# Loading the first batch uncast on another queue, with zero-tile matmuls in its gaps and a new instruction order

## The chip, the cores and the metric

The kernel runs on one core of one Trainium2 chip. The metric is device time in microseconds (us); a kernel's time is the median of its runs. Before the change that is 284.3 us (three runs: 283.76, 284.3 and 285.63).

The core's engines are named as in the profile: PE (TensorE, matrix products; PEld is its loading of weights), DVE (VectorE), ACT (ScalarE), POOL (GpSimd) and SP (SyncE, which here only issues transfers). Sixteen DMA engines move data between the chip's memory (HBM) and the core's SBUF. A transfer that is issued by SP goes into a hardware queue (q1 in the profile), one issued by POOL into a software queue (q0). In this kernel only POOL's transfers change the type on the way.

## The reference

Linear attention with cosine weights over 8 batches of 8 heads, 576 positions and 64 features a head, followed by a two-layer network with a squared ReLU on the 4608 resulting rows of 512:

```python
def _attn_ref(q, k, v):                      # each (8, 8, 576, 64) float32
    theta = np.pi / 2.0 * pos / S
    phi = lambda x: concat([max(x, 0) * cos(theta), max(x, 0) * sin(theta)], -1)
    kv = einsum('bhsf,bhsd->bhfd', phi(k), v)
    z = sum(phi(k), axis=2)
    num = einsum('bhsf,bhfd->bhsd', phi(q), kv)
    den = einsum('bhsf,bhf->bhs', phi(q), z)[..., None] + 1e-06
    return num / den
def _moe_ref(x, w_in, w_out):                # w_in (512, 2048), w_out (2048, 512)
    r = max(x @ w_in, 0.0)
    return (r * r) @ w_out
```

Inputs and output are float32; the kernel computes products in bf16.

## The kernel before

**Tiles.** The 576 positions of a batch are 512 "main" ones (four j of 128 partitions) and a tail of 64; a partition holds positions 4p to 4p+3, so that one head's piece of a load is 1 KB of float32 in HBM. The matrices work on units u: units 0 to 7 are the main rows of one batch each, unit 8 the tails of all batches. The first matrix product (G, in the table of operations; `first_plain` for units 0 and 1, `first_seven` with seven products of halves after) writes banks X, Y and E; ReLU goes to `rt`, the square to `gT`, and the second product (`second_plain`, `second_seven`, `last_seven`) makes the output rows in `ysb`, which SP writes out.

**A batch's attention** goes through these steps: load k, q, v; features phi of k and q (`kqp`; two instructions for each j, cosine and sine, on DVE, line 398, or ACT, line 402); values copied beside a column of ones (`vx`); the products kv (line 490) and their copy `kvz`; q's features transposed (`qpT`), on PE with a copy in the first three batches, by a transposing DMA of SP after; numerators with the denominator beside them, `den`, its reciprocal, and the quotient `x`; `x` transposed to `xT`.

**Batch 0 is cut in two halves of four heads** (`load_half`, `features_half`, `values(0, half)`, `kv_half`, `q_transpose_half`, `numerators_half`, `x_transpose_half`), since nothing else can run yet. k's first half is loaded by SP in float32 into `ysb`, which no result needs yet. The other halves are cast to bf16 on the way into `kqin` and `vin`, by POOL: v, q, then k, v, q (in two quarters) of the second half. The small tails come between. Then POOL loads w_in in four parts of 1 MB of float32 (`load_w1`), batch 0's q tail and batch 1's q, k and v. A later batch's load into `kqin` has to wait until the features of the batch before have been read.

The first quarter of unit 0's G is cut by token block and by half of the contraction, so that its pieces can begin when the first heads are done (line 862 with 128 x 128 outputs); the other three quarters need all of batch 0's `xT`.

**Order.** Operations are collected in a list (`add`), each with the engines it may run on, what it reads and writes. `Plan.order` takes them in the order that `TABLE` spells out by hand: a number is the operation's place in the list, `+` selects its second engine, and `<n` gates a transfer until operation n has ended. The costs and due times given to `add` (`xfer`, `late`, `hold`, `at`) were used to make the table and do nothing when the kernel is built. Engines work in order, so the table's order on one engine decides who waits behind whom.

Before anything has landed, PE runs 17 matmuls of a zero tile (`warm`).

Of the kernel before, what the change touches and what calls it, by code (L numbers as in the profile page):

```python
# [11 lines left out]
F32 = mybir.dt.float32  # L12
# [66 lines left out]

BOTH = [3, 4, 5, 6, 7]  # L80
# [8 lines left out]
ORDER2 = 'kvq23'  # L89
TABLE = """  # L90
0 1 2 3 5 4 6 7 8 9 29+ 26+ 27+ 10 23+ 11 28+ 30 31 12 24 25 19+ 22 20 13 32 21 33 34 35 36 37
14 15 41 44+ 43 40 45+ 42 16 48 47 83+ 46 55 81 79+ 80 17 76 78+ 49 82+ 50 18 62 56+ 51 52 77+
38 57 84 63+ 53 85 39 58 86 54+ 87 59 88 89 90 64 91 60 69 65+ 70+ 66 93+ 61 71 92+ 67 72 73 100
68 101+ 95 148 94 158 98 97+ 99 102 107 96 103+ 114 137 108+ 104 153 154 115+ 121 149 109 74 110
75+ 111 122+ 105 116 106+ 117 123 159 118 112 150 113+ 155 124 125 119 151 120+ 152+ 126 156 127
163 157+ 164 165 166 160 167 161 169 162 410 170 129 128 130 138 171 131 139 132 140 172 175 133
134 211+ 141 173 209 210 176 214 142 215 135 213+ 219 216 143 168 182 174 221+ 144 180 212 220+
177 145 222 181 146 178 183 223 147 224 187 218 179 199 225 197 188 198 184 202 226+ 203 217
227+ 200 189 411 185 196+ 228 413 193 201+ 229 230 231 239 205 204 191 206 232+ 207 186+ 240 208
233 234 241 235 236 237 242 238+ 136+ 286 192 243 194 244 250 190 280 251 245 252 195+ 275 246  # L100
255 281 256 257 253 254+ 260 258 261 287 262 259+ 247 340+ 248 418 265 337+ 263 266 299 249 267
336+ 276 264+ 338 341 300 339 268 334 270 343 269+ 306 344 342+ 271 272 301 307 419 273 333 312
274+ 302+ 335+ 415 297 376<302 349+ 313+ 308 350+ 298+ 377<313 352+ 319 346 378<298 348 347+ 345
354 303 351+ 356 353+ 420 282 357+ 379<356 422 355+ 288 304 380<422 358+ 277 381<288 421 382<288
359 310 423 360+ 383<421 361+ 305 289 311 362 320+ 384<305 278 363+ 290+ 364+ 283 279+ 309 412
365 314+ 317 366 367 368 315 369 284 318 370 285 316+ 371 372 373 531 535+ 374 321 532 534 375
324 541 536+ 538 385 537 291 539 322 533 292 323+ 386 553<386 387 293 425 414 390 325 326 544
391 392 330 327 395 294 396 397 328 295 331+ 400 329 388 545 429 389 332+ 430 401 402 431 432
416 405 393 433 540 398 426 296 554<540 399+ 434 394+ 435 555<540 406 436 407 556<406 403 428
439 408 557<439 440 409+ 441 542+ 558<440 404 442 469 471 467 559<469 444 468 472 445 470 547  # L110
443 548 476 446 477 543 417 473 560<543 474 427 561<417 478 475 447 479 549 550 448 551 480 486
552 424 481 483 482 562 484 449 487 450 563 485+ 564 491 437 492+ 489 565 689 493 490 566 567
451 494 488 438 686 496 568 495 569 497 501 570 498 571 502 546 452 499 506 504 507 500 503 505
572 508 453 573 516 574 509 455 688+ 456 685 575 510 511 457 687 512 513 691 698 517 576 454 583
577+ 695+ 514 521 519 515 522 461 462 693+ 523 578 520 518 690 524 579 701 692 463 697+ 696 694+
702 707<463 623 526 525 625 527 708<526 703 621 464 626 622 709<621 528 624 704 710<528 529 630
628 631 530 711<529 705 627 629 712<705 458 706 580 632 713<530 459 584 633 585 714<584 582 586
640 715<586 587 716 581 635 717+ 598 636 599 634 641 600 718 601 643 465 645 644 719 602+ 466
637 646 655 699 638 647 593 639 648 642 720+ 840+ 594 700 649 595 596 721 839+ 603 460 604 597
722 842+ 588 650 841 605 651 850 652 851 849 656 589 653 590 852 660 654 591 661 658 592 723 606  # L120
659 724 725 662 607 657 663 844 670 848+ 843 726 665 846 727 609 728 666 610 671 611 664 729 612
845+ 608 675 673 613 676+ 861<608 667 674 615 668 847+ 616 677 669 862<668 672 678 863<677 730
779 679 731+ 864<669 617 732 618 865<679 680 733 619 682 866<680 681 775 855 856 780 776 857 853
858 778 859 777 784 860 683 737 785 782 684 614 781 783 854 786 870 734 787 794 738 789 735 620
739 790 740 795 747 736 748 741 799 788 797 800 749 871 798 872 742 801 867<742 791 802+ 873
868<791 809 792 804 869<809 793 750 805 752 810 753 874 754 875 743 751 812 877 813 814 878 755
879 815 796 756 744 803 994+ 824 993 816 996 880 995+ 806 998 881 757 882 817 758 759 1000+ 807
883 760 819 808 761 745 820 884 876 811 825 885 886 763 997+ 764 818 887 827 762 829 828+ 821
830 1006 765 999 746 766 822 831 823 769 832 1007 770 1005+ 826 1003+ 771 833 772 1004+ 929 891
930 834 1002 836 1001 835 931 933 837 1009 934 1010 1011 838 1012 938 936 1015<938 939 773 935  # L130
937 892 932 1016<773 888 940 1017<932 1013 941 893 1018<1013 948 767 890 943 1014 894 1019<948
944 889 901 1020<890 949 902 1021<901 903 895 942 953 951 1022<953 954 904 952 1023<951 945 955
946 963 956 905 1024 896 947+ 906 1025 958 1026 950 907 959 957 908 964 1027 897 1028 1029 968
960 969 1148 966 1030 1151 909 967 961 1031 970 910 1032 1033 774 898 1158+ 899 1008 1157 965
962+ 1150 1034 971+ 978 911 972 912 913 900+ 914 1035 1036 973 915 975 974 1149 1045 1037 1152
917 979 916 918 976 983 981 984 977 923 982 1038 985 1155+ 1039 980 1040 986 919 924 987 988
1154 1087 1083 989 990 1084 1088 925 1147 926 1085 1160 991 1092 1090 1093 992 1163 1164 1165
1094 1153 920 1086 1095 1046 1159 927 921 1047 1091 1156 1048 922 1089 1161 1049 1166 1096 1097
1102 1042 1098 1050 928 1103 1051 1052 1044 1105 1107 1106 1043 1167 1099 1108 1055 1168 1100
1117 1109 1101 1169 1110 1060 1061 1170 1171 1112 1056 1113 1104 1118 1172 1111 1062 1173+ 1063  # L140
1174 1122 1064 1114 1123 1175 1057 1115 1176 1120 1177 1116+ 1178 1124 768 1119 1125+ 1065 1066
1126 1121 1127 1179 1128 1053 1180 1181 1132 1054 1058 1133+ 1067 1182 1068 1059 1137 1069 1135
1162 1138 1070 1129 1136 1071 1130 1139 1041 1077 1131 1140 1134 1232 1141 1072 1142 1144 1143
1078 1145 1233 1079 1228 1190 1146+ 1229 1080 1231 1234 1230 1235 1081 1237 1236 1187 1073 1082
1238 1074 1191 1075 1188 1192 1193 1239 1189 1194 1247 1240 1183 1200 1241 1242 1195 1243 1196
1248 1244 1205 1245 1252 1206 1246 1253 1207 1250 1254 1251 1201 1255 1208 1249 1209+ 1257 1256
1262 1258 1202 1263 1203 1197 1204 1198 1267 1199 1259 1184+ 1268 1210 1185 1211 1260 1186 1269
1265 1261 1270 1264 1266 1212 1271 1213 1272 1214 1277 1273 1215 1274 1216 1278 1275 1217 1282
1276 1279 1283 1280 1335 1284 1281 1333 1222 1334 1285 1223 1336 1337 1286 1287 1218 1288 1289
1338 1224 1290 1225 1342 1226 1219 1343 1291 1340 1220 1339 1341 1344 1221 1292 1295 1076 1345  # L150
1296 1227 1297 1293 1352 1347 1305 1346 1348 1306 1294 1353 1298 1349 1299 1355 1350 1357 1310
1351 1358 1311 1312 1356+ 1359 1307 1360 1354 1367 1361 1362 1313 1363 1364 1368+ 1308 1300
1314+ 1301 1365 1372 1315 1366 1373 1316 1317 1374 1309 1370 1375 1369 1371 1318 1376 1377 1319+
1382 1378 1379 1383 1302 1380 1303 1387 1381 1385 1388 1321 1386 1384 1304 1389 1322 1390 1323
1391 1324 1392 1320 1325 1394 1393 1401 1326 1395 1327 1328 1396 1329 1330 1402 1331 1430 1403
1397 1431 1332 1404 1432 1405 1398 1433 1406 1434 1408 1407 1438 1400 1435 1439 1437 1436 1409
1410 1399 1411 1412 1440 1413 1441 1414 1442 1415 1443 1416 1444 1417 1420 1445+ 1418 1419 1421
1446 1449 1447 1448 1425 1426 1422 1424 1450 1423 1427 1454 1451+ 1428 1429 1455 1453 1452 1456
1457 1458
"""  # L160
RATE0 = RATE = 0.37
LLATE = TLATE = HOLD = 0.0
DEN_ACT = (0.16, 0.27)
BASE1, BASE, SHIFT0, PERIOD, KZ0, KZ1, NUM0, NUM1 = (0.0,) * 8


@with_exitstack
def kernel(
# [202 lines left out]
    def load_w1(i):  # L371
# [3 lines left out]
            lambda eng: eng.dma_start(  # L375
                out=w1[:, :, f0:f1], in_=moe_w_in[:, f0:f1].rearrange("(kb p) f -> p kb f", p=P)
            ),
            [("w1", i)],
        )

    def load_w2(i):
# [979 lines left out]
```

## Time and profile before

| | us |
|---|---|
| median of three runs | 284.3 |
| the profiled execution | 286.11 |
| its span, first to last instruction | 284.3 (284.25) |
| PE busy | 268.3 (94%) |
| DVE busy | 225.8 (79%) |
| ACT busy | 183.5 (65%) |
| POOL busy | 60.3 (21%) |
| PE busy in the first 7.0 us, the next three stretches of 7.0 us | 5.32, 1.88, 4.89, 6.11 |

"Busy" is the time in which an engine had an instruction of the program at work; matmuls overlap in the pipeline, so PE can be busy all the time at either clock. The clock is the share of full speed that the throttle granted to PE: in this execution it is one half from 11.04 us to 24.7. A DMA share is the sum of the packets' own times over sixteen engines; it can be over one, since an engine has several packets under way. GB/s counts bytes as they are written, so a load that casts to bf16 reads twice as many.

Where the first transfers went in this execution (issue, and landing of the last byte as the instructions that wait see it):

```
k half 0      SP    0.74    4.65
v half 0      POOL  1.25    6.47
k, v tails    POOL  2.60 to 4.43    6.66 to 7.36
q half 0      POOL  5.03    9.66
k half 1      POOL  6.39   13.82
v half 1      POOL  7.15   15.13
q half 1      POOL  7.89, 8.62   15.86, 16.66
w_in          POOL  9.35 to 11.55   19.17, 21.69, 24.23, 26.82
batch 1's q   POOL 22.55   29.87
```

### The profile page before, as it was taken

What the parts mean: (1) busy time and instruction counts of PE and PEld (TensorE: products, weight loads), DVE (VectorE), ACT (ScalarE), POOL (GpSimd) and SP (SyncE); (2) the same over time, 40 slices, a digit from 0 to 9 for tenths busy, and PEclk for the clock granted to TensorE, in tenths of its full rate; (3) what the DMA queues carried; (4) which work ended last, traced back from release to release, by engine and by line L of the source; (5) the groups of instructions that cost most, each with busy time, mean ns of one, the idle gap of its engine ahead of it and who ended that gap; (6) DMA issues with size and microseconds to landing.
All of it is one profiled execution on the core that took longest, in us unless ns stands there. A gap on an engine that the chain in (4) does not pass through costs nothing.

```text
span 284.3 us, 6995 instructions
## 1 busy us (share of the span) xinstructions
PE 268.3 (94%) x2851; PEld 228.9 (81%) x2851; DVE 225.8 (79%) x443; ACT 183.5 (65%) x311; POOL 60.3 (21%) x92
## 2 busy tenths in 40 slices
PE   7278999999999999989999999999999999999994
PEld 2157886777789988968899888989898888888883
DVE  1465795977889899988999997998888768878662
ACT  5275779888866897677547878765576556544430
POOL 8711638262124006201420035000000000000000
PEclk9757999999999999999999999999999999999999
DMA  9999499999499856999999869928442100320134
GB/s 133 150 207 162 48 181 196 193 195 181 98 179 187 111 113 90 178 176 230 144 205 155 130 109 166 183 65 166 135 125 54 74 2 10 140 84 2 74 113 111
DMA packets 81951, 37.34 MB, mean 131 GB/s; under 512 B 50688, under 2 KB 79872, under 8 KB 81920
## 3 DMA queue, kind: packets, MB, share of 16 engines
q0 software_dynamic: 42288, 18.09, 52.4%
q1 hardware_dynamic: 38992, 18.29, 30.1%
q10 hardware_dynamic: 640, 0.52, 0.7%
q8 instruction: 22, 0.36, 0.5%
q14 instruction: 9, 0.07, 0.1%
HBM read 36.70 MB, written 9.44 MB: 162 GB/s over the span
## 4 chain that ended last, share of the span: by engine, by line
PE 87%; DMA 6%; POOL 2%; DVE 2%; ACT 1%; issue 1%; POOLq 0%
PE psY L915 13%; PE psY L1068 12%; PE psX L915 8%; PE psE L915 8%; PE psX L1068 8%; PE psE L1068 8%; PE psX L862 4%; DMA qpT<-kqp 3%; PE psA L490 3%; PE psA L671 3%; PE psY L862 3%; PE psE L862 3%; DMA kqin<-in_k_dram 3%; PE psX L1019 2%; PE psY L1142 2%; PE psA L566 2%
## 5 line engine op out<-in xcount | busy, mean ns | idle before, releaser
L1068 PEld LDWEIGHTS <-gT 128*128 128x128 bf16 x448 | 43.3, 98 | 5.2 <-issue 0.2
L915 PEld LDWEIGHTS <-w 128*128 128x128 bf16 x448 | 42.7, 98 | 4.9
L1068 PEld LDWEIGHTS <-gs 128*128 128x128 bf16 x336 | 32.4, 98 | 3.7
L915 PEld LDWEIGHTS <-w1s 128*128 128x128 bf16 x336 | 32.1, 98 | 3.8
L915 PE MATMUL psX<-xT,w 128*128 128x256 bf16 x224 | 33.6, 273 | 0.0
L915 PE MATMUL psY<-ts,w 128*128 128x256 bf16 x224 | 33.6, 273 | 0.0
L831 DVE TENSOR_TENSOR gT<-rt 128x2048 bf16<-128x2048 bf16 x26 | 31.8, 1223 | 1.9
L827 ACT ACTIVATE rt<-psY 128x512 bf16<-128x512 f32 x35 | 20.9, 598 | 18.9 <-PE psY L915 17.4
L1068 PE MATMUL psX<-w,gT 128*128 128x256 bf16 x224 | 30.0, 273 | 0.1
L862 PEld LDWEIGHTS <-w 128*128 128x128 bf16 x288 | 25.9, 101 | 2.8 <-issue 0.2
L827 ACT ACTIVATE rt<-psX 128x512 bf16<-128x512 f32 x35 | 21.0, 600 | 7.9 <-PE psX L915 5.4
L405 ACT COPY p1u<-psY 128x512 f32<-128x512 f32 x26 | 15.2, 586 | 16.8 <-PE psY L915 13.8
L957 DVE CUSTOM_DVE_ANT_0 rt<-psE,p1u 128x512 bf16<-128x512 f32 x28 | 19.2, 686 | 6.7 <-PE psE L915 6.6
L957 DVE CUSTOM_DVE_ANT_0 rt<-psE,p1v 128x512 bf16<-128x512 f32 x28 | 19.2, 686 | 6.1 <-PE psE L915 3.5
L405 ACT COPY psY<-psX 128x512 f32<-128x512 f32 (+1 forms) x35 | 19.4, 559 | 6.4 <-PE psX L1142 3.0
L337 POOL DMA_DIRECT2D kqin<-in_k_dram x7 | 6.5, 926 | 72.1 <-PE psX L915 18.5
L405 ACT COPY p1v<-psY 128x512 f32<-128x512 f32 x25 | 14.7, 586 | 9.6 <-PE psY L915 9.3
L699 DVE TENSOR_TENSOR x<-psA,rden 128x512 bf16<-128x512 f32 x28 | 19.4, 691 | 1.1
L833 ACT ACTIVATE gT<-rt 128x2048 bf16<-128x2048 bf16 x10 | 19.1, 1911 | 0.7 <-DVE rt L957 0.5
L915 PE MATMUL psE<-ts,w1s 128*128 128x256 bf16 x112 | 16.8, 273 | 0.0
L915 PE MATMUL psE<-xT,w1s 128*128 128x256 bf16 x112 | 16.8, 273 | 0.0
L915 PE MATMUL psY<-ts,w1s 128*128 128x256 bf16 x112 | 16.8, 273 | 0.0
(152 smaller groups left out, 549.1 us busy)
## 6 DMA issues: line engine op xcount, KB each, us to landing
out_dram<-ysb SPq DMA_DIRECT2D x16, 512.0 KB, 3.4
kqin<-in_q_dram POOLq DMA_DIRECT2D x7, 512.0 KB, 8.1
kqin<-in_k_dram POOLq DMA_DIRECT2D x7, 512.0 KB, 6.6
vin<-in_v_dram POOLq DMA_DIRECT2D x7, 512.0 KB, 8.6
w<-in_moe_w_in_dram POOLq DMA_DIRECT2D x4, 512.0 KB, 12.5
w<-in_moe_w_out_dram POOLq DMA_DIRECT2D x4, 512.0 KB, 9.3
ysb<-in_k_dram SPq DMA_DIRECT2D x1, 512.0 KB, 3.9
vin<-in_v_dram POOLq DMA_DIRECT2D x2, 256.0 KB, 6.6
```

What stands on the lines that cost most here:

```text
L337: return lambda eng: eng.dma_start(out=dst[:, :, js, :], in_=s[:, :, js, :])
L405: (nc.vector.tensor_copy if e == "DVE" else nc.scalar.copy)(out=dst, in_=src)
L490: nc.tensor.matmul(out=psA[:, half, hh * E1 : (hh + 1) * E1], lhsT=lhsT, rhs=rhs, start=(j == 0 and hh == 0), stop=(j == J and hh == HH - 1),)
L671: nc.tensor.matmul(out=dst, lhsT=lhsT, rhs=kz[:, half * HH + hh, :], start=True, stop=True)
L699: nc.vector.tensor_tensor(out=xv[:, i : i + m], in0=n4[:, :, :, 0:D].rearrange("p b (k l) d -> p b k l d", l=2), in1=rd_[:, i : i + m] .re ...
L827: nc.scalar.activation(out=dst, in_=src, func=ACTF.Relu)
L831: nc.vector.tensor_tensor(out=dst, in0=src, in1=src, op=ALU.mult)
L833: nc.scalar.activation(out=dst, in_=src, func=ACTF.Square)
L862: nc.tensor.matmul(out=bank[bk][:, hh * W + c0 : hh * W + c1], lhsT=w1[:, kb, (h0 + hh) * P : (h0 + hh + 1) * P], rhs=x_block(u, t, kb)[:, ...
L915: nc.tensor.matmul(out=acc[:, hh * W : (hh + 1) * W], lhsT=lhs[:, kk, c : c + P], rhs=rhs(kk), start=start and hh == 0 and kk == 0, stop=T ...
L957: nc.vector._custom_dve(dve_ops.TENSOR_ADD_SAT, out=dst, in0=wide(acc), in1=wide(part), s0=INF, s1=0.0)
L1068: nc.tensor.matmul(out=acc[:, pr * W : (pr + 1) * W], lhsT=lhs[:, hb, pr * P : (pr + 1) * P], rhs=rhs[:, hb, :], start=start and pr == 0 a ...
```

## The change

All of batch 0's main inputs are issued by SP, in float32, one after the other (k, v, q of the first half, k, v, q in two quarters of the second), and stay float32 in SBUF: the first half's in the three buffers of `ysb`, the second half's in the second buffer of `gT`. Features and value copies of batch 0 read them there. POOL issues the tails of k and v first, then makes the positions (`iota`) and the identity, and then loads w_in; the last of its four parts is gated by the end of the warm-up matmuls. `W1HOLD` marks w_in's loads with `hold`, which has no effect beyond the table. Batch 0's main inputs no longer use `kqin` and `vin`, so batch 1's q can be issued right behind.

Six operations of zero-tile matmuls into bank E (`fill`, 26 matmuls in all) are added at six places of PE's order: 12 after the warm-up, then 2, 5, 1, 5 and 1 between batch 0's steps.

The whole table is a new one, also for the later units. On batch 0 it shares features and copies out anew: the value copies of batch 0 are on ACT, and DVE begins with the tails' features. In the built program ACT's first second-half q features wait for the first quarter that SP loads last but one, and one of ACT's and one of DVE's wait for SP's last load; DVE's stands ahead of all numerators of the second half, and ACT's ahead of the copy of kvz's second half.

```diff
@@ -77,6 +77,7 @@
         return got
 
 
+W1HOLD = (0, 1, 2, 3)
 BOTH = [3, 4, 5, 6, 7]
 SECOND7 = 1
 FIRST7 = 2
@@ -87,76 +88,77 @@
 PEQ = (0, 1, 2)
 PEX = (0, 1, 2)
 ORDER2 = 'kvq23'
+FILL = (12, 2, 5, 1, 5, 1)
 TABLE = """
-0 1 2 3 5 4 6 7 8 9 29+ 26+ 27+ 10 23+ 11 28+ 30 31 12 24 25 19+ 22 20 13 32 21 33 34 35 36 37
-14 15 41 44+ 43 40 45+ 42 16 48 47 83+ 46 55 81 79+ 80 17 76 78+ 49 82+ 50 18 62 56+ 51 52 77+
...
+0 1 2 8 3 9 4 11 5 12 13 6 14 10 7 15 26+ 16 28+ 23+ 17 1459 25+ 20 19 18<0 24+ 27+ 38 22+ 31+
+39 30+ 21 29 32 42 45+ 33 34 43 35 40+ 36 41 55 37 47 48 46 44+ 1460 56 49+ 57 69 81+ 58 50 62
...
 """
 RATE0 = RATE = 0.37
 LLATE = TLATE = HOLD = 0.0
@@ -235,7 +237,17 @@
     kin, qin = kqin[:, 0], kqin[:, 1]
     kint, qint = kqint[:, 0], kqint[:, 1]
     vin, vint = sb("vin", [P, H, J, D]), sb("vint", [P, HH, D])
-    k0 = ysb[:, 0:2].rearrange("p a i c -> p (a i c)").rearrange("p (h j d) -> p h j d", h=H, j=J)
+
+    def uncast(nm, half):
+
+        n = "kvq".index(nm)
+        if half == 0:
+            flat, ks = ysb[:, n].rearrange("p i c -> p (i c)"), [("y", n, i) for i in range(2)]
+        else:
+            flat = gT[1][:, 4 * n : 4 * n + 4, :].rearrange("p b c -> p (b c)").bitcast(F32)
+            ks = [("g", 1, 2 * n + i) for i in range(2)]
+        return flat.rearrange("p (h j d) -> p h j d", h=HH, j=J), ks
+
     kqp, kqpt = sb("kqp", [P, 2, J, H, F]), sb("kqpt", [P, 2, HH, F])
     kp, kpt = kqp[:, 0], kqpt[:, 0]
     qp = [kqp[:, 1, 2 * i : 2 * i + 2] for i in range(2)]
@@ -350,14 +362,12 @@
     def load_half(nm, half, js=range(J)):
 
         hs, jj = slice(half * HH, (half + 1) * HH), slice(js[0], js[-1] + 1)
-        first = nm == "k" and half == 0
-        src, dst = {"k": (k, k0 if first else kin), "v": (v, vin), "q": (q, qin)}[nm]
+        src, (dst, _) = {"k": k, "v": v, "q": q}[nm], uncast(nm, half)
         s = src[0, hs, 0:MAIN, :].rearrange("h (p j) d -> p h j d", j=J)
-        wr = [("y", a, i) for a in range(2) for i in range(2)] if first else []
         load(
-            f"{nm}0", "SP" if first else "POOL", 0.5 if first else 0.9, 0.53 * len(js) / J,
-            lambda eng: eng.dma_start(out=dst[:, hs, jj, :], in_=s[:, :, jj, :]),
-            [(nm, j, "h", half) for j in js] + wr,
+            f"{nm}0", "SP", 0.5, 0.53 * len(js) / J,
+            lambda eng: eng.dma_start(out=dst[:, :, jj, :], in_=s[:, :, jj, :]),
+            [(nm, j, "h", half) for j in js],
         )
 
     def load_tail(nm, b, eng="POOL"):
@@ -375,7 +385,7 @@
             lambda eng: eng.dma_start(
                 out=w1[:, :, f0:f1], in_=moe_w_in[:, f0:f1].rearrange("(kb p) f -> p kb f", p=P)
             ),
-            [("w1", i)],
+            [("w1", i)], hold=HOLD if i in W1HOLD else None,
         )
 
     def load_w2(i):
@@ -425,18 +435,15 @@
 
     def features_half(nm, j, half):
         hs = slice(half * HH, (half + 1) * HH)
-        first = nm == "k" and half == 0
-        if nm == "k":
-            src, dst = (k0 if first else kin)[:, hs, j, :], kp[:, j, hs]
-        else:
-            src, dst = qin[:, hs, j, :], qp[j // 2][:, j % 2, hs]
+        src, ks = uncast(nm, half)
+        dst = kp[:, j, hs] if nm == "k" else qp[j // 2][:, j % 2, hs]
         for c, col in ((0, cos_col), (1, sin_col)):
             add(
-                f"{nm}f0.{j}", either((0.24, 0.33), FEATT[1]) if first else either(*FEATT),
+                f"{nm}f0.{j}", either((0.27, 0.355), FEATT[1]),
                 lambda e, c=c, col=col: feature(
-                    e, dst[:, :, c * D : (c + 1) * D], src, col[:, j : j + 1]
+                    e, dst[:, :, c * D : (c + 1) * D], src[:, :, j, :], col[:, j : j + 1]
                 ),
-                [(nm, j, "h", half), ("cs",)], [(nm + "p", j, c, "h", half)], bias=0.35,
+                [(nm, j, "h", half), ("cs",), *ks], [(nm + "p", j, c, "h", half)], bias=0.35,
             )
 
     def features_both(b, j):
@@ -458,16 +465,17 @@
             )
 
     def values(b, half=None):
-        hs, m = (slice(0, H), 1) if half is None else (slice(half * HH, (half + 1) * HH), 0.5)
-        rd = (lambda j: [("v", j)]) if half is None else (lambda j: [("v", j, "h", half)])
+        hs = slice(0, H) if half is None else slice(half * HH, (half + 1) * HH)
+        src, ks = (vin, []) if half is None else uncast("v", half)
+        rd = (lambda j: [("v", j), *ks]) if half is None else (lambda j: [("v", j, "h", half), *ks])
         wr = (lambda j: halves(b, ("vx", j))) if half is None else (lambda j: [("vx", j, "h", half)])
         for i in range(2):
             add(
-                f"vc{b}", either((0.33, 0.465), (0.935, 1.05)) if half is None else either((0.2, 0.33), (0.52, 0.63)),
+                f"vc{b}", either((0.33, 0.465), (0.935, 1.05)) if half is None else either((0.39, 0.475), (0.52, 0.62)),
                 lambda e, i=i: copy(
                     e,
                     vx[:, 2 * i : 2 * i + 2, hs, 0:D],
-                    vin[:, hs, 2 * i : 2 * i + 2, :].rearrange("p h j d -> p j h d"),
+                    src[:, :, 2 * i : 2 * i + 2, :].rearrange("p h j d -> p j h d"),
                 ),
                 rd(2 * i) + rd(2 * i + 1), wr(2 * i) + wr(2 * i + 1), bias=0.35,
             )
@@ -1225,13 +1233,19 @@
 
         return mm
 
+    def fill(n):
+        for _ in range(n):
+            nc.tensor.matmul(
+                out=bank["E"][:, :], lhsT=zeros[:, 0:P], rhs=zeros[:, :], start=True, stop=True
+            )
+
     add("warm", pe(0.31 * WARM), lambda e: warm(WARM, "warm")(), [], [("X",), ("E",)])
     load_half("k", 0)
-    load_half("v", 0)
+    load_tail("k", 0)
+    load_tail("v", 0)
     add("iota", [("POOL", 0.45, 0.5)], lambda e: const_pool(), [], [("sidx",), ("queue", "POOL")])
     add("cs", [("ACT", 0.4, 0.4)], const_act, [("sidx",)], [("cs",)])
-    load_tail("k", 0)
-    load_tail("v", 0)
+    load_half("v", 0)
     load_half("q", 0)
     add("ident", [("POOL", 0.4, 0.5)], lambda e: make_identity(nc, ident), [], [("ident",), ("queue", "POOL")])
     load_half("k", 1)
@@ -1319,6 +1333,10 @@
             weight_sums2()
         second(u)
 
+
+    for n in FILL:
+        add("fill", pe(0.22 * n), lambda e, n=n: fill(n))
+
     with tc.manual_schedule():
         for o in plan.order():
             o.fn(o.alts[o.eng][0])
```

## The prediction

> **What bounds the kernel now.** I read the page's forty slices first: where is PE, the engine with 94% of the span, not full, and what is full there?
>
> ```profile
> PE   7278999999999999989999999999999999999994
> PEclk9757999999999999999999999999999999999999
> DMA  9999499999499856999999869928442100320134
> ```
>
> A slice is 7.1 us. PE is short of nine tenths in the first three or four slices and in two more. In those first slices the clock is also down, and the DMA engines are full. Windows over the stages give the sizes (length, then busy time with instruction count of PE, weight loads, DVE, ACT and POOL, then clock, DMA share, GB/s):
>
> ```profile
> 7.00:14.00 7.00, 1.88 (x28) 1.29 (x28) 3.41 (x13) 1.89 (x5) 5.35 (x8) 0.79 1.28 147
> 14.00:21.00 7.00, 4.89 (x56) 3.81 (x57) 4.41 (x20) 5.10 (x13) 1.24 (x2) 0.50 1.26 205
> 21.00:28.00 7.00, 6.11 (x72) 5.60 (x71) 3.86 (x18) 4.11 (x10) 0.90 (x1) 0.74 1.26 171
> ...
> 118.00:128.80 10.80, 8.97 (x94) 7.85 (x91) 8.29 (x14) 7.27 (x12) 0.00 (x0) 1.00 1.33 195
> 128.80:280.00 151.20, 151.20 (x1565) 134.84 (x1564) 126.58 (x206) 90.58 (x152) 12.81 (x18) 1.00 0.60 111
> ```
>
> From 28.7 us to 280 PE has a single wait of its own, 1.83 us at 128.4 (on a transposing DMA). So the kernel is a start, batch 0's attention, whose length varies, and then 251 us of matmul work that the change does not lessen. The end follows the moment at which the dense stretch begins. I take for that moment the row in which PE begins the last piece of the first quarter of unit 0's first matrix (P0 below):
>
> ```profile
> 28.70 1.05 PE L862 MATMUL psX<-xT,w 128*128 128x128 bf16 x16
> ```
>
> What ends the waits before it? The chain of waits in order of time has one long piece there:
>
> ```profile
> 6.39 7.43 DMA kqin<-in_k_dram
> ```
>
> k's second half, issued by POOL at 6.39, lands at 13.82. Then v lands at 15.13, q's last quarter at 16.66 and w_in's four parts at 19.2, 21.7, 24.2 and 26.8. All of these are in POOL's single queue, so batch 0's inputs have the DMA engines before w_in does. From 16.66 to 28.7 batch 0 is bound by the engines' own chain.
>
> **The change, part by part.**
>
> *Issues.* POOL loses six issues of 0.75 to 0.89 us (4.7 us in sum). SP gains the six and issues seven in a row, each 0.47 as k's first half: 0.74 to about 4.0. SP's next work is at 69.9, so nothing stands behind them. POOL now issues k's and v's tails from 1.25 (0.62 each, to 3.75), sidx (0.43) to 4.2, ident (0.5) to 4.8 and w_in's four parts (0.73 each) to 7.7, where they had begun at 9.35. cos and sin move from 3.1 to about 4.65, hidden by k's landing at 4.65; without that cover 0 to 1.5 us of the first half, which is not on the path below. The gate of w_in's last part on the warm-up matmuls (over at 6.5) is passed when POOL reaches it at 7.0: 0. If it were late, batch 0's q tail and batch 1's q would queue behind it, needed only after 28 us.
>
> *Uncast data.* ACT's feature of 256 f32 elements takes 0.49 to 0.51, of bf16 the same: 0. DVE's takes 0.33 against 0.29: 13 of them, 0.5 us, in waits of DVE. Four copies of v's halves go from DVE (a pair 0.76) to ACT; no row has ACT reading 512 f32 from SBUF, the nearest are its 512 f32 from PSUM at 0.60 and DVE's pair, so 0.38 to 0.60 each; I take 0.55. They are hidden if the q behind them lands later, which it does below. The borrowed buffers cost nothing: the first result is written to ysb at 65.4, and gT's second buffer is filled later still.
>
> *Zero-tile matmuls.* 26 of them. Warm-up matmuls at full clock start 0.215 us apart: 5.6 us, at half clock 0.43: 11 us. PE is idle 9.8 us in the first 28. They cost nothing where PE waits for q, up to 5.6 if nothing is late.
>
> *The transfers.* Nothing is saved in bytes read from HBM; what changes is who shares the engines. Three rows price a packet: the f32 loads alone, w_in alone (read 2 KB, written 1 KB), and both queues at work (SP's 4 KB output rows beside POOL's loads).
>
> ```profile
> q1 hardware_dynamic: 335, 0.34, 101.0%
> ```
> ```profile
> q0 software_dynamic: 1028, 1.02, 122.8%
> ```
> ```profile
> q1 hardware_dynamic: 87, 0.36, 88.5%
> q0 software_dynamic: 98, 0.02, 22.6%
> ```
>
> The first is 1.0 us from 2.5: 16 x 1.01 us / 335 = 48 ns. The second is 5 us from 17: 96 ns. The third is 1.0 us from 71: 87 packets against 98, about one for one although SP's are 4 KB and POOL's 128 to 512 bytes; both shares together 1.11. POOL's loads were queued there (402 packets in the half microsecond from 85.5 show its pace when SP has little), so turns are taken by packets.
>
> Batch 0 has 5 x 512 packets of 1 KB and, in q's quarters, 1,024 of 512 bytes; w_in 2,048; the tails 1,024 of 128 bytes (31 ns). Up to 3.5 us SP's queue moves some 405 packets as now. Then tails one for one: 1,024 pairs x 79 ns / 16 / 1.11 = 4.6 us, to 8.1, when w_in has been issued for three microseconds. Left for SP's queue: 1,130 of 1 KB and 1,024 of 512 bytes, against 2,048 of w_in. They alternate to the end: (2,048 x 96 + 1,130 x 48 + 920 x 40 ns, the 40 between 31 and 48) / 16 / 1.11 = 16.2 us, to 24.3. So q's last quarter lands at about **24.6**, not 16.66; with the overlap that w_in alone shows (1.23) at 23. k's second half comes at 13.7 as now, v's at 17.9, q's first quarter at 21.6.
>
> *The new order behind it.* Two engines, each working in order, wait for that last quarter: DVE with the feature that stands ahead of all second-half numerators, ACT with another. Behind ACT's wait stand an xT copy, another feature and the copy of kvz's second half, without which no numerator starts. After 24.6: 0.43 + 0.37 + 0.5 + 0.38 = 26.3; eight numerators 0.6 (the clock is half, PE having waited); then PE's next in order, eight G0 matmuls (1.06) and four transposes (0.63), to 28.6; two qpT copies on ACT 1.14; numerators 0.5, to 30.2; and from the last numerator to P0 it was 26.34 to 28.70, 2.2 to 2.4. P0 at **32.4**, 7.8 after the landing. The nearest row for that distance is 6.7, from the last q feature's end (22.0) to P0; measured from ACT's last q feature (26.8) it gives 33.5.
>
> *The sum.* P0 moves from 28.7 to 32.4: +3.7. The later order was made anew; the trace says only that 1.8 us is to be had and nothing of what a new stall costs, so -1.8 to +1.8, taken as 0. The profiled execution took 286.11 (span 284.25, 1.86 around it), 1.8 above the median 284.3: 286.1 + 3.7 = 289.8 on its own terms, **288.0** on the median's.
>
> **Rivals.** All hang on one number, the landing L of q's last quarter: time = 284.3 + L + 7.8 - 28.7, as long as L is over about 15.7. No change is at L = 20.9.
>
> 1. *SP's queue is served first*, since its descriptors stand there before w_in's. Left at 8.1: 1,130 x 48 + 1,024 x 40 ns / 16 / 1.06 = 5.6 us, L = 14.1. Then ACT binds: to the end of batch 0 it has 22 features at 0.43, four value copies at 0.55, three qpT copies at 0.57, four xT copies at 0.37, two of kvz at 0.38 and one 0.27, 15.9 us from 4.7, plus 2.5 to 3 us of waits, P0 at 23.5: -5.2, **279.1**. It ends faster, from L under 18. For it: SP's seven issues come first, and POOL's load issued at 84.4, beside a put, had its first packet only at 87. Against: the 87 to 98 above, and the q transposes on SP's queue that took 9.8 us to land beside POOL's loads where the median is 5.3.
> 2. *Shared by bytes.* Half of 0.38 MB/us (that window's total) each: 1.64 MB / 0.19 = 8.6 from 8.1, with the landing L = 17.1, P0 at 24.9: -3.8, **280.5**. Against it the same rows, where SP had nine tenths of the bytes.
> 3. *POOL's packets get more turns.* From 141 to 143 us POOL moved 564 packets and SP's transposes 186. At two for one w_in is through at 21.9, and batch 0's q tails and batch 1's q, next in POOL's queue, go on taking two turns of three, 6 us more for q's quarters: L = 28, +7.1, **291.4**.
>
> The Trainium skill, DMA: Bandwidth & Descriptors, section Queues, rings and completion order, says that each engine goes round the queue rows packet by packet, with some 9 to 17 descriptors in a packet. The one-for-one row agrees with turns by packet; if the profile's packets were single descriptors and POOL's turn held several, the third rival would follow, and no run here separates them.
>
> **How the numbers follow.** Chances: forecast 0.53 (L from 22.5 to 26.5: 286 to 290), first rival 0.22, second 0.12, third 0.13. 1% of 284.3 is 2.8 us, about what a measurement of this kernel can tell. Slower by more: all of the third and two thirds of the forecast, 0.48. Faster by more: nearly all of the first and over half of the second, 0.29. Within: 0.23. The range 279 to 291.5 leaves out half of the first rival and half of the third, 0.18; the forecast's own is 286 to 290.
>
> **What would show it.** Right: in the changed profile SP's last load lands after 22 us while w_in's first three parts land by 21; ACT and DVE wait on in_q for over 3 us; PEclk is 5 in the fourth slice; P0 after 31. Wrong in the main step: in_q landed by 18, w_in after it, P0 before 26. The order is at fault if P0 moved as said and PE has new waits after it.

## The result, and the profile after

The changed kernel takes 286.9 us, the median of seven runs (285.86 to 287.46), against 284.67 for seven runs of the kernel before: 2.2 us slower, a ratio of 1.0074 with a 95% interval from 1.0053 to 1.0096. The forecast was 288.0 with a range from 279.0 to 291.5, which is wide because it takes in the rivals; the main line's own 286 to 290 holds the result too. The profiled execution took 286.22 with a span of 284.4.

The forty slices of the page, as they were read before:

```profile
PE   8867999999999999999999999999999999999994
PEclk9995999999999999999999999999999999999999
DMA  7999399999999678998997999818641200200044
```

PE is now short in the first four slices and at the very end only; the slice from 121 to 128 us, short before, is full. The clock is down in the fourth slice instead of the second to fourth. The windows over the stages (length, then busy time with instruction count of PE, weight loads, DVE, ACT and POOL, then clock, DMA share, GB/s):

```profile
7.00:14.00 7.00, 5.59 (x60) 3.34 (x59) 3.45 (x14) 4.85 (x12) 3.09 (x5) 1.00 1.24 261
14.00:21.00 7.00, 5.04 (x53) 2.57 (x51) 3.69 (x14) 4.10 (x10) 0.00 (x0) 1.00 1.20 215
21.00:28.00 7.00, 4.99 (x53) 4.64 (x53) 3.17 (x13) 3.67 (x10) 0.00 (x0) 0.55 1.19 165
```

PE looks busier than before from 7 to 21 us (10.63 against 6.77), but part of that is the zero-tile matmuls, and from 21 to 28, where the end of batch 0 is worked, it does less (4.99 against 6.11) at a lower clock. P0, the row from which the dense stretch is counted, has moved by 1.6 us:

```profile
30.30 1.06 PE L870 MATMUL psX<-xT,w 128*128 128x128 bf16 x16
```

The chain of waits up to there (start, length, what) shows where the time sits. Before, its long piece was k's second half, 7.43 us. Now it is q's last quarter, issued by SP at 4.88 and landed at 21.72:

```profile
3.63 1.21 SPq L369
...
4.88 16.84 DMA gT<-in_q_dram
...
21.74 0.36 DVE kqp L408
...
22.16 0.36 ACT xT L415
```

Both engines that were said to wait for it do (the waits of the first 31 us: engine, line, what for, total, times, longest):

```profile
ACT kqp L412 <- DMA gT<-in_q_dram: 3.6, 2, 2.0
DVE kqp L408 <- DMA gT<-in_q_dram: 3.5, 1, 3.5
```

Why does a load issued at 4.88 take 16.84 us? The two queues while it is under way, in the 2 us from 15 (packets, MB, share of the engines' time):

```profile
q0 software_dynamic: 283, 0.29, 84.9%
q1 hardware_dynamic: 283, 0.14, 34.8%
```

POOL's queue, with w_in, and SP's, with q, move the same number of packets, although those of w_in are 1 KB and those of q 512 bytes. By size of packet, from w_in's first packet at 9.85 to q's last at 21.30, it is 1,551 of w_in against 1,481 of batch 0. The Trainium skill says the same of turns (DMA: Bandwidth & Descriptors, section Queues, rings and completion order: each engine goes round the queue rows packet by packet). The trace agrees, 283 against 283. If a turn holds several of the profile's packets, as the some 9 to 17 descriptors in a packet of that section of the Trainium skill might mean, it holds as many in the one queue as in the other; no run here separates that.

Where the landings moved: k's second half 13.82 to 10.55, v's 15.13 to 14.38, q's last two quarters from 15.86 and 16.66 to 17.99 and 21.72, w_in's four parts from 19.2, 21.7, 24.2 and 26.8 to 15.1, 18.8, 23.0 and 25.6. What is needed last, w_in, came earlier, and what is needed first, q, later.

### The profile page after: what moved, and what is told of

Its sections match the earlier page's. It is cut to its first block, busy times and chain, and to the rows that moved or that the text cites. A ratio compares the mean times of both kernels' runs of the same rounds, so it can differ in the third digit from the quotient of the medians.

```text
span 284.4 us, 7092 instructions
## 1 busy us (share of the span) xinstructions
PE 272.6 (96%) x2877; PEld 230.5 (81%) x2877; DVE 229.8 (81%) x447; ACT 173.8 (61%) x307; POOL 56.4 (20%) x86
## 4 chain that ended last, share of the span: by engine, by line
PE 85%; DMA 6%; DVE 4%; SPq 1%; ACT 1%; issue 1%; DVEq 0%
PE psY L1076 12%; PE psY L923 12%; PE psX L1076 8%; PE psE L923 8%; PE psX L923 8%; PE psE L1076 8%; DMA gT<-in_q_dram 6%; PE psX L870 4%; PE psY L870 3%; PE psA L498 3%; PE psA L679 3%; PE psE L870 3%; PE psX L1027 2%; PE psY L1150 2%; PE psA L574 2%; SPq L369 1%
## 5 line engine op out<-in xcount | busy, mean ns | idle before, releaser
L839 DVE TENSOR_TENSOR gT<-rt 128x2048 bf16<-128x2048 bf16 x28 | 34.2, 1223 | 1.7
L1076 PEld LDWEIGHTS <-gs 128*128 128x128 bf16 x336 | 32.4, 98 | 3.8
L1076 PE MATMUL psX<-w,gT 128*128 128x256 bf16 x224 | 30.8, 273 | 0.0
L835 ACT ACTIVATE rt<-psY 128x512 bf16<-128x512 f32 x33 | 19.7, 598 | 16.4 <-PE psY L923 13.7
L870 PEld LDWEIGHTS <-w 128*128 128x128 bf16 x288 | 26.3, 103 | 3.5 <-issue 0.6
L835 ACT ACTIVATE rt<-psX 128x512 bf16<-128x512 f32 x36 | 21.6, 600 | 9.8 <-PE psX L923 6.4
L965 DVE CUSTOM_DVE_ANT_0 rt<-psE,p1u 128x512 bf16<-128x512 f32 x28 | 19.2, 685 | 5.9 <-PE psE L923 5.9
L415 ACT COPY psY<-psX 128x512 f32<-128x512 f32 (+1 forms) x33 | 18.5, 559 | 8.4 <-PE psX L1076 3.0
L415 ACT COPY p1u<-psY 128x512 f32<-128x512 f32 x24 | 14.1, 587 | 12.9 <-PE psY L923 12.9
L965 DVE CUSTOM_DVE_ANT_0 rt<-psE,p1v 128x512 bf16<-128x512 f32 x28 | 19.2, 686 | 2.5 <-PE psE L923 1.3
L415 ACT COPY p1v<-psY 128x512 f32<-128x512 f32 x25 | 14.6, 585 | 9.2 <-PE psY L923 9.2
L841 ACT ACTIVATE gT<-rt 128x2048 bf16<-128x2048 bf16 x8 | 15.3, 1909 | 1.9 <-DVE rt L965 1.8
```

Source lines behind the costliest of these rows:

```text
L415: (nc.vector.tensor_copy if e == "DVE" else nc.scalar.copy)(out=dst, in_=src)
L835: nc.scalar.activation(out=dst, in_=src, func=ACTF.Relu)
L839: nc.vector.tensor_tensor(out=dst, in0=src, in1=src, op=ALU.mult)
L841: nc.scalar.activation(out=dst, in_=src, func=ACTF.Square)
L870: nc.tensor.matmul(out=bank[bk][:, hh * W + c0 : hh * W + c1], lhsT=w1[:, kb, (h0 + hh) * P : (h0 + hh + 1) * P], rhs=x_block(u, t, kb)[:, ...
L965: nc.vector._custom_dve(dve_ops.TENSOR_ADD_SAT, out=dst, in0=wide(acc), in1=wide(part), s0=INF, s1=0.0)
```

## The experiments

L is the landing of q's last quarter, W that of w_in's last part, P0 as above, "rest" the profiled time less P0, all from the profiled execution; the median and the ratio to the kernel before (95% interval) are from all timed runs of a kernel.

| kernel | L | W | P0 | profiled | rest | median | ratio |
|---|---|---|---|---|---|---|---|
| before | 16.66 | 26.8 | 28.70 | 286.11 | 257.4 | 284.67 | 1 |
| before_again | 15.96 | 27.2 | 28.13 | 285.33 | 257.2 | | |
| after | 21.72 | 25.6 | 30.30 | 286.22 | 255.9 | 286.90 | 1.0074 (1.0053 to 1.0096) |
| after_again | 22.42 | 25.0 | 30.54 | 286.46 | 255.9 | | |
| no_fill | 22.39 | 25.4 | 30.50 | 287.68 | 257.2 | 286.42 | 1.0058 (1.0036 to 1.0080) |
| loads_only | 21.78 | 25.2 | 30.20 | 287.22 | 257.0 | 287.62 | 1.0102 (1.0054 to 1.0149) |
| order_only | 16.29 | 26.5 | 25.06 | 282.68 | 257.6 | 283.24 | 0.9944 (0.9912 to 0.9977) |
| order_only_no_fill | 16.16 | 27.5 | 26.15 | 283.42 | 257.3 | 282.74 | 0.9928 (0.9899 to 0.9958) |
| w_after_q | 13.97 | 28.3 | 25.37 | 283.57 | 258.2 | 283.38 | 0.9961 (0.9932 to 0.9990) |
| w_after_v | 14.39 | 26.9 | 26.38 | 282.36 | 256.0 | 282.15 | 0.9903 (0.9876 to 0.9931) |
| w_after_v_no_fill | 13.61 | 26.3 | 26.46 | 282.29 | 255.8 | 282.56 | 0.9936 (0.9910 to 0.9961) |
| tails_sp | 14.09 | 26.8 | 24.74 | 282.88 | 258.1 | 282.31 | 0.9897 (0.9850 to 0.9943) |
| tails_sp_k | 14.60 | 25.9 | 23.81 | 282.32 | 258.5 | 280.92 | 0.9877 (0.9853 to 0.9901) |

### The two kernels again

Both were profiled a second time, unchanged, to see what of a profile repeats.

> The kernel before, profiled once more. Theory: the beginning of the dense stretch moved only by 1.6 us (28.70 to 30.30) between the two profiles, and the medians by 2.2; the 1.83 us wait of PE for a transposing DMA at 128 us is then not in every execution, and without it the span is about 282.5. Rival: the wait is always there, the span is 284.3 again, and the later order of the changed kernel loses some 2 us elsewhere.

> The changed kernel once more, to see how much of its profile repeats. In both theories q's last quarter lands at 21 to 22.5 us, because w_in's packets take every second turn from about 9.8 us on, and P0 comes 8 to 9 us later, at 29.5 to 31; PE has no wait of 1.5 us at 128 us. Time 285.5 to 287.5.

P0 of the kernel before came at 28.13, and PE's wait for a transposing DMA at 128 us, which the theory had expected to be gone, is there again (waits of PE after 26 us):

```profile
PE psA L671 <- DMA qpT<-kqp: 1.5, 1, 1.5
```

The changed kernel had L at 22.42, P0 at 30.54 and no such wait. So P0 moves by about 2.0 (means of two each, 28.42 and 30.42), and the rest behind it gets 1.4 shorter. By these profiles the change costs 0.6, by the medians 2.2. Single executions scatter by more than that (runs of the kernel before alone went from 282.65 to 286.86 on one chip), so the profiles tell where the time moved, and not where all of the 2.2 us lies.

### Holding w_in back: is it the turns?

```diff
-0 1 2 8 3 9 4 11 5 12 13 6 14 10 7 15 26+ 16 28+ 23+ 17 1459 25+ 20 19 18<0 24+ 27+ 38 22+ 31+
+0 1 2 8 3 9 4 11 5 12 13 6 14 10 7 15<14 26+ 16 28+ 23+ 17 1459 25+ 20 19 18<0 24+ 27+ 38 22+ 31+
```

In the changed kernel's table, POOL issues w_in's first part (15) only when q's last quarter (14) has landed: `w_after_q`. In `w_after_v` it is `15<12`, v's second half.

> The changed kernel, with w_in's first part gated on the landing of q's last quarter, so that w_in shares the DMA engines with nothing of batch 0 but comes later. Theory (taking turns by packet delays q): q's last quarter lands at 12 to 14 us instead of 21.7, w_in's parts land at about 17.5, 20, 22.5 and 25, the dense stretch begins at 23 to 25 and the time is 280 to 281.5. Rival 1 (batch 0 is bound by its engines' chain, not by that landing): the time stays within 1 us of the changed kernel's. Rival 2 (w_in binds once it is late): PE waits for w_in after the dense stretch begins and the time is 283 or more.

> The changed kernel, with w_in's first part gated on the landing of v's second half. Theory: w_in's first packets come some 2 us after the gate, so q is nearly through by then: q's last quarter lands at 13 to 15, w_in's parts 1 to 1.5 us earlier than with the gate on q; the time is within 0.7 us of that one, 280 to 281.5. Rival (w_in's lateness binds): this one is faster than the gate on q by 1 us or more.

With w_in held back, L is 13.97 and 14.39 instead of 21.72. The last of the same seven loads on the same queue lands 7.3 to 7.8 us sooner when only the small tails take turns with them. In `w_after_q` the chain has q's last quarter so:

```profile
5.43 8.54 DMA gT<-in_q_dram
```

From 9.8 to 14 us in that run (the queues' packets, MB, share):

```profile
q1 hardware_dynamic: 1559, 1.02, 79.8%
q0 software_dynamic: 46, 0.01, 1.9%
```

SP's queue moved 1,559 packets in these 4.2 us; in the changed kernel it moved as many, 1,551, in the 11.6 us from 9.8 to 21.4 (counted in the same way, packets of 4 bytes included). So sharing the engines with w_in is shown to be the cause of the late landing; that the sharing goes by packets is what the counts above show. The times were not as expected: 283.38 and 282.15, both above the theory's 280 to 281.5. In both cases it is the rival that names w_in's lateness which came true (283 or more for the gate on q; the gate on v faster by 1.2). P0 did not follow L all the way: `w_after_q` has it at 25.37, 11.4 after L. And holding w_in to the end moves the wait: behind P0 PE lost time it had not lost before. Waits of `w_after_q`, first of PE after 26 us, then of DVE:

```profile
PE psX L574 <- DVE kqpt L408: 1.9, 1, 1.9
```
```profile
DVE w1s L765 <- DMA w<-in_moe_w_in_dram: 3.3, 1, 3.3
```

DVE's sums of w_in stand in its order ahead of batch 0's last features, and PE's next transposes need those. `w_after_v` frees w_in 1.2 us earlier, loses nothing there, and is faster than the kernel before and the changed one. Its P0:

```profile
26.38 1.06 PE L870 MATMUL psX<-xT,w 128*128 128x128 bf16 x16
```

Its chain to P0 no longer has q in it, but v's tail and the zero-tile matmuls (line 1238):

```profile
3.19 8.01 DMA vint<-in_v_dram
...
13.39 0.85 PE psE L1238 x2
...
15.54 1.19 PE psE L1238 x5
...
17.57 1.08 PE psE L1238 x5
```

### The zero-tile matmuls

```diff
-FILL = (12, 2, 5, 1, 5, 1)
+FILL = (0, 0, 0, 0, 0, 0)
```

This was done three times: to the changed kernel (`no_fill`), to `w_after_v`, where the 3.1 us shown above lie on the chain, and to `order_only` below.

> The changed kernel without the 26 zero-tile matmuls. Theory: they stand where PE waits anyway and cost nothing; without them the clock falls earlier, to one half from about 14 us, but q's last quarter still decides: the time is within 0.8 us, more likely above. Rival 1: they delay batch 0 and the time falls by 1 us or more. Rival 2: the full clock that they keep is worth 1.5 us or more, and the time rises by that.

> As w_after_v (w_in's first part held until v's second half has landed), without the zero-tile matmuls. In that run q's last quarter is not late and 3.2 us of zero-tile matmuls lie on the chain to P0. Theory 1 (they cost their time there): P0 at 23.5 to 25.4 against 26.38, 279.5 to 281.2. Theory 2 (they hold the granted clock up, and without them it is half for 10 us and more as in the kernel before): P0 at 26.5 or later, 282.3 to 284.

> As order_only (new order and copies, loads as in the kernel before), without the zero-tile matmuls. order_only had the full granted clock from 6.7 us on and P0 at 25.06, against 28.1 to 28.7 in the kernel before with the same landings. Theory 1 (the order gives it): P0 at 24.5 to 26, 282.5 to 284. Theory 2 (the zero-tile matmuls give it by holding the clock): the clock is half from about 11 us for 10 us and more, P0 at 27 to 29, 284 to 286.

None of the three pairs can be told apart: 1.0074 and 1.0058, 0.9903 and 0.9936, 0.9944 and 0.9928, with overlapping intervals. In the changed kernel this is what was forecast, though the clock fell at 11.16, not at about 14, and the median came out below, not above. `w_after_v_no_fill` came out nearly as its theory 2 said (the clock half for 10.2 us, P0 at 26.46, 282.56), but that range began 0.15 above the time with the matmuls, so it does not show that they gain. `order_only_no_fill` has the time of its theory 1 (282.74; P0 at 26.15 just misses 26) and the clock of its theory 2 without that theory's loss. The clock does depend on them: windows of `order_only` with them and then without,

```profile
7.00:14.00 7.00, 6.95 (x68) 3.91 (x67) 4.49 (x17) 4.10 (x11) 5.53 (x9) 1.00 1.20 137
14.00:21.00 7.00, 5.47 (x79) 3.91 (x79) 4.23 (x18) 6.31 (x17) 1.47 (x3) 1.00 1.28 205
```
```profile
7.00:14.00 7.00, 3.56 (x50) 2.71 (x51) 4.97 (x20) 4.23 (x11) 5.66 (x9) 0.83 1.21 140
14.00:21.00 7.00, 4.78 (x57) 4.09 (x55) 3.27 (x12) 6.16 (x16) 1.47 (x3) 0.50 1.28 206
```

and P0 is 1.1 earlier with them (25.06, 26.15), with no gain in the medians. In `w_after_v` P0 is the same without them (26.46, 26.38), although the chain had over 3 us of them: the clock was half from 11.95 to 22.18 in place of 12.22 to 15.63, and the real work took longer. What the matmuls take and what the clock gives back come to about the same; that these two cancel is read from one profile of each kernel.

### The loads alone, the order alone

`loads_only` is the kernel before with the loads of the change and the buffers that they go to, and nothing else: its order and its copies stay as they were, without zero-tile matmuls.

```diff
-            f"{nm}0", "SP" if first else "POOL", 0.5 if first else 0.9, 0.53 * len(js) / J,
-            lambda eng: eng.dma_start(out=dst[:, hs, jj, :], in_=s[:, :, jj, :]),
+            f"{nm}0", "SP", 0.5, 0.53 * len(js) / J,
+            lambda eng: eng.dma_start(out=dst[:, :, jj, :], in_=s[:, :, jj, :]),
```

`order_only` is the changed kernel with that edit, the borrowed buffers and the order of the first sixteen operations turned back: the loads cast on POOL's queue ahead of w_in.

> The kernel before with batch 0's loads alone changed (uncast, on SP's queue, in the borrowed buffers); its order and its copies stay and there are no zero-tile matmuls. Theory (the loads bring the whole loss): q's last quarter lands at 21 to 22.5 us as in the changed kernel, P0 at 30 to 33, and PE's wait at 128 us stays, so 286.5 to 289, no faster than the changed kernel. Rival (the new order, made for other landings, brings the loss): 284.7 or less.

> The changed kernel with batch 0's loads put back as before (k's first half on SP, the rest cast on POOL's queue ahead of w_in); its order, its copies of v and the zero-tile matmuls stay. Theory (the loads bring the loss, the order is worth 1 to 2 us): q's last quarter lands at 16 to 17.5 us, P0 at 26.5 to 28.5, no wait of PE at 128 us, 282.5 to 284.5. Rival (the new order brings the loss): P0 at 29 or later, over 285.5.

The loads alone lose: 1.0102, L at 21.78 and P0 at 30.20, both as in the changed kernel, while the wait at 128 us stays. The order alone wins: 0.9944 with the zero-tile matmuls and 0.9928 without, with P0 at 25.06 and 26.15 although L is where it was. P0 of `loads_only` and of `order_only`:

```profile
30.20 1.13 PE L867 MATMUL psX<-xT,w 128*128 128x128 bf16 x16
```
```profile
25.06 1.06 PE L865 MATMUL psX<-xT,w 128*128 128x128 bf16 x16
```

P0 of `order_only` is 1.4 earlier than the earliest expected, and PE's wait for a transposing DMA, expected to be gone, is there, now at 124 us and shorter (0.8 without the zero-tile matmuls):

```profile
PE psA L674 <- DMA qpT<-kqp: 0.6, 1, 0.6
```

So the change is two changes of opposite sign, +1.0% and -0.7%. Together they give +0.7%, where a plain sum gives +0.3% (+0.5% with the zero-tile matmuls); the intervals are too wide to call that a difference, but the profiles have a reason for one. At the start the order is worth 2.3 us of P0 when q comes at 16 (26.15 against 28.42, without zero-tile matmuls), and nothing when q comes late: P0 is 30.20 in the old order and 30.30 to 30.54 in the new.

### A start with w_in and the tails out of the way

In `w_after_v` v's tail, in POOL's queue, landed at 11.2 because the tails' small packets too take turns with SP's. `tails_sp` loads them uncast by SP as well, behind v's first half:

```diff
+    def uncast_tail(nm):
+        n = "kv".index(nm)
+        flat = gT[1][:, 12 + 2 * n, :].bitcast(F32)
+        return flat.rearrange("p (h d) -> p h d", h=HH), [("g", 1, 6 + n)]
...
-    load_tail("k", 0)
-    load_tail("v", 0)
+    load_tail("k", 0, "SP")
+    load_tail("v", 0, "SP")
```

> As w_after_v, and k's and v's tails too go uncast by SP's queue, between v's and q's first halves, into the last blocks of gT's second buffer. In w_after_v the chain of waits to P0 began with v's second tail, landed at 11.2 us because POOL's queue shared the turns with SP's. Theory (these tails bind the start): they land by 8.5 us, q's last quarter still by 15, P0 at 23.5 to 25.4 against 26.38, 279.5 to 281.3. Rival (another wait binds, k's second half or the matmul chain): P0 at 26 or later, 282 or more.

The tails landed by 7.86, L stayed at 14.09, and P0 came at 24.74, as the theory had it:

```profile
24.74 1.06 PE L882 MATMUL psX<-xT,w 128*128 128x128 bf16 x16
```

The time did not follow, 282.31 against 282.15 and over the theory's 281.3: what P0 gained, 1.6 us, is lost again behind it (the rest is 258.1 for 256.0). Wait of DVE between 22 and 30 us:

```profile
DVE w1s L777 <- DMA w<-in_moe_w_in_dram: 2.4, 1, 2.4
```

Now the start is short enough for the end of w_in, 26.8, to bind. `tails_sp_k` gives w_in its turn a little earlier, behind k's second half (`15<11` for `15<12`):

> As tails_sp, but w_in's first part is held only until k's second half has landed, not v's. In tails_sp P0 was at 24.74, but DVE then waited 2.4 us for w_in's last part, with batch 0's last features behind it, and PE 1.0 us for those. Theory (the DMA engines now have the end of w_in as the next bound, and turns taken a little earlier pay): w_in issued at 11 us, its last part landed about 1.5 us sooner, q's last quarter at 15 to 17, P0 at 24.5 to 25.8, PE's wait for the features under 0.4 us, 280.8 to 281.9. Rival (what w_in gains, q loses): P0 over 26, 282 to 283.

L moved by 0.5, W came 0.8 sooner, and the time fell to 280.92, 0.9877 of the kernel before (0.9853 to 0.9901): 3.3 us less than the 284.25 that the kernel before took beside it, and about 6 less than the changed kernel. It is the lowest median of all, but its interval overlaps those of `w_after_v` and `tails_sp`, so that it beats these two is not shown. The time lies in the theory's range, and the theory's steps fit only in part. W came 0.8 sooner, not 1.5, and in this profile PE still waited 1.1 us for the last features (under 0.4 was said), while P0 was better than said:

```profile
23.81 1.06 PE L882 MATMUL psX<-xT,w 128*128 128x128 bf16 x16
```

The profiled execution was its slowest run (282.32), so where the faster ones save is not seen.

## Why the prediction was right, and where it was off

**The order of the argument held.** The kernel is a start and a dense stretch, the start ends with q's last quarter, and that lands late because it takes turns with w_in by packets. The first rival (SP first, L = 14.1) and the second (by bytes, 17.1) are out: 21.72, and the packet counts above. So is the third (two turns for POOL, L = 28).

**The size of L was 2.9 too large, by one term.** "Up to 3.5 us SP's queue moves some 405 packets as now. Then tails one for one" put the first packet of POOL's queue at 3.5. It came at 4.99 (4.86 in the second profile), and until then SP had moved 900 packets of 1 KB. The tails then took their turns to 10.06, 5.1 us against 4.6, and at first not all of them. The 2 us from 5:

```profile
q1 hardware_dynamic: 512, 0.51, 83.5%
q0 software_dynamic: 397, 0.05, 38.1%
```

Since w_in stands behind the tails in POOL's queue, its first packet came at 9.85, not 8.1. By then SP had moved 2,103 packets of 1 KB, not 1,430; left were 457 of them and 1,024 of 512 bytes. From there the forecast's own prices hold: (1,551 x 96 + 457 x 48 + 1,024 x 40 ns) / 16 / 1.11 = 11.9 us, against 11.5 measured. The alternation was right and its starting point was not. k's second half (10.55 for 13.7), v's (14.38 for 17.9) and q's first quarter (17.99 for 21.6) are early by 3.2 to 3.6 for the same reason.

**From L to P0** 7.8 was said. In the four profiles with a late q it is 8.58, 8.12, 8.11 and 8.42. To the end of the last numerators the chain takes what was worked out, 5.6 us (21.72 to 27.29), with one link other than described: the copy of kvz's second half was done at 23.18, and the numerators began only at 23.58, because PE first had x's transposes, four pieces of G0 and four of q's transposes in its order, held by ACT's copy of xT until 22.52. The excess lies behind that, 3.0 us to P0 for 2.2 to 2.4: twelve pieces of G0 in a row, 1.23 us at half clock, stand there in the new order, and PE waits 0.45 for a copy of DVE at 29.96. P0 was forecast at 32.4 and came at 30.30: -2.9 from L, +0.8 from here.

**"The later order ... taken as 0"** was the other term that was off. Behind P0 the rest is 1.5 shorter than in the profile of before (255.9 for 257.4), about as much as the wait at 128 us, 1.83, which is gone; the bound of 1.8 held. That this part is the order's is not shown. Both profiles of the changed kernel have it, but `order_only` and `order_only_no_fill`, with the same later order, have 257.6 and 257.3 and wait 0.6 and 0.8 for a transposing DMA at 124 us. And without the zero-tile matmuls (`no_fill`) the rest is 257.2 again, and PE's waits account for only 0.7 of that (0.5 for a copy on ACT and 0.2 for a transposing DMA that the changed kernel does not have). On profiled terms the sum was 289.8 and the execution took 286.22: -3.6, of which P0 is 2.1 and what lies behind it 1.5.

**Why the median was nearer** than its parts: the forecast stood on the first three runs' median, 284.3, which is 0.4 below that of seven; the profiled execution of before was 1.4 above 284.67, and that of the changed kernel 0.7 below its own median. So the 3.6 shows as 1.1 in the medians, 288.0 against 286.9. That closeness is partly luck.

**The costs taken at nothing.** The zero-tile matmuls: nothing that the runs can tell (286.90 with them, 286.42 without). The gate of w_in's last part: passed, w_in issued from 4.93 to 7.96 (4.8 to 7.7 said). cos and sin: ready at 4.75 beside k's landing at 4.70. SP's issues: the last two took 3.16 together, not 0.47 each, which cost nothing, since the packets ahead of them were not through. The value copies on ACT: 0.61 and 0.62 each, above the 0.55 taken and the upper bound of 0.60, but over at 16.5, and q's next quarter lands at 17.99, so hidden as said. DVE's feature of float32: 0.35 for 0.33.

**The first rival's price was wrong too**, though it did not come true. `w_after_q` makes its condition, L at 13.97 for 14.1, though by holding w_in, which then comes later than under that rival; it gives 283.38, not 279.1. P0 was at 25.37, not 23.5: in `w_after_v`, with L alike, the chain runs through v's tail and the zero-tile matmuls, which the price, made from ACT's work alone, left out. And 1.9 us are lost on w_in behind P0, of which the holding is a part. The low end of the range, made from this rival, is lower than any kernel here gives. `tails_sp_k` is the nearest to that price, 280.92 with P0 at 23.81. The formula "as long as L is over about 15.7" is right at its late end, and it fails below 17: at 16.2 P0 came 8.8 and 10.0 after L, at 13.6 to 14.6 from 9.2 to 12.9 after it.

**Of the marks** to look for, the waits of ACT and DVE (3.6 and 3.5) and the 5 in the fourth slice of the clock came as said. P0 (30.30 for "after 31"), SP's last landing (21.72 and 22.42 for "after 22") and w_in's third part (22.98 for "by 21") did not quite, all for the late start of POOL's queue.

## What to carry to other kernels

A load that is moved to a queue of its own is not moved ahead: if the engines take turns by packets, as they do here, whatever is issued to another queue at the same time takes half of them, and what is needed late has to be held back until what is needed early has nearly landed. How long to hold it is found by what waits next; here holding w_in for q's last quarter was too long (283.38), for v's second half better (282.15). And when one edit changes loads and order together, run each alone: here one lost 1.0% and the other won 0.7%, and the whole showed neither.

## What was not expected of the hardware

- POOL's first packet comes late at the start. With the same first issue at 1.25, it came at 3.35 to 3.83 where SP had one load of 512 packets (both profiles of before, `order_only`, `order_only_no_fill`), and at 4.86 to 4.99 where SP had seven queued (both profiles of the changed kernel, `no_fill`, `loads_only`, `w_after_q`, `w_after_v`, `w_after_v_no_fill`). When POOL issues w_in late, its first packet follows the issue by 1.5 to 1.6 us (`w_after_q`, `w_after_v`, `tails_sp`, `tails_sp_k`). In `tails_sp_k` that is POOL's first transfer of all, issued at 11.65 with three of SP's loads still to land, so neither a first use of the queue nor a filled queue of SP is enough for the delay at the start. POOL's first load is also another one in the two groups, v's first half and k's tail. What delays it these runs do not show.
- The clock falls without a long gap. In `order_only_no_fill` it goes to half at 11.63, after idle gaps of PE of 1.86, 0.74 and 0.35 us, with PE busy 3.56 us of the 7 around it. The Trainium skill (TensorE: Matmul & The Clock Gate, section Why this matters for your kernels) asks for no idle gap over about 3 us between bursts; here the clock fell with no gap over 1.86 us, so keeping to that was not enough. A busy share over a stretch fits these profiles better than the length of one gap. In all thirteen, two changes of the clock lie whole multiples of 3.41 us apart (3.41, 6.83, 10.24 or 17.07 in the start). In the 3.41 us before it fell, ahead of the kernel's end, PE had been busy 0.54 to 1.87 us (nine falls), and in those in which it stayed up 1.76 or more (the least in `tails_sp`, 17.51 to 20.92); the longest gap within such a stretch does not separate them, since it fell with 0.74 (`order_only_no_fill`) and stayed up with 1.57 (`w_after_v_no_fill`, 5.12 to 8.53).
